# A spectral mixing layer with a gated MLP: the second-half sums of pair 0 move into the MLP, the first unit is reordered, statistics are issued sooner, and the DFT blocks get another layout

## The chip, the cores and the metric

The kernel runs on one core of a Trainium2 chip. The metric is the device time of one execution in microseconds; of several executions the median is taken.

## The reference

All arrays are fp32. x has 2048 rows (positions) of 512 values, F is 1792.

```python
xn = _layernorm(x, axis=-1)                       # eps 1e-5
a = einsum("bsd,ed->bse", xn, dft_hid_re)
b = einsum("bsd,ed->bse", xn, dft_hid_im)
s = einsum("ts,bse->bte", dft_seq_re, a) - einsum("ts,bse->bte", dft_seq_im, b)
g = sigmoid(einsum("bsd,df->bsf", xn, w_gate)) * einsum("bsd,df->bsf", xn, w_up)
out = x + s * silu(einsum("bsf,fd->bsd", g, w_down))
```

## The kernel before

Every matrix product is made of three fp32r products: each operand is split into a high part (a copy rounded to fp32r, on ScalarE, `high`, L120 or L373) and a low part (the operand less its high part, on VectorE, `make` or `low`, L125 or L376), and `mm3` adds high by high, low by high and high by low in PSUM. Large products are blocked two by two with seven products in place of eight (k = 1 to 7 in the code), at the price of sums and differences of blocks, on VectorE (`combine`, L129) or by adding DMAs.

The work runs in this order. First the transform along the sequence, in four chunks of 512 output positions (`Chunk`, t = 0 to 3); the hidden dimension follows later, at the end. Then the MLP, as 14 blocks of seven units for two halves of the positions (`block`, `Down`, `Seven`). Then the transform along the hidden dimension for two pairs of chunks (`hidden_units`), which multiplies the result by the gate and adds it to the output. Between them partial results stand in DRAM: f_raw (four blocks for each chunk), f_sum (sums of f_raw blocks of a pair of chunks, which `hidden_units` loads), g_part (the MLP's).

`units` is the list of all units of TensorE work. A unit of the sequence transform is 12 matmuls of 128x512; an MLP unit is 12, or 18 with a down product. The order is written by hand: for each unit n the loop at the end of the kernel issues what was hung on n by `sooner`, starts the loads of the units up to n + 5 (LOAD_AHEAD) and the splits of those up to n + 2 (SPLIT_AHEAD), then what hangs on n by `amid`, the unit itself, and what hangs on it by `after`. Each engine works through its own instructions in the order in which they are issued. All loads (`Load.load`, L81) go through SyncE's queue (SP), all stores and adding DMAs through GpSimd's. All tiles in SBUF that hold data are taken from one pool of 54 pages of 512 KB; a load whose page is still in use waits on its queue, with all behind it.

The first 24 units are products 1 and 2 of chunks 0 to 2 in turn (t runs fastest, then the pair of row blocks pp = 0 to 3). Their left operand is x normalised: `stats(0, pp)` finds mean and variance of a 128x2x512 tile on VectorE (L178, L179, L171) and the moments on GpSimd (L172 to L174, the one at L173 is a power of -0.5), `normed` (L370) normalises with them on ScalarE. e = 0, 1 are the two halves of a tile along its contraction; pair 0 and 1 are done in `begin`, pairs 2 and 3 by `prepare`, hung on units 6 and 9. Unit 0 has its own order of matmuls, in `Chunk.run`.

`n` in the driver is 112, the first unit of the MLP, so `f_sums(0, 1, n - 35, 2)` hangs four steps (L730: a sum on VectorE and its store) on units 77, 79, 81 and 83, with their loads of f_raw three units before. Units 84 to 111 are chunk 3. `x_norm` makes the transposed, normalised x of the MLP in the same time.

Of the kernel before, what the change touches and what calls it, by code (L numbers as in the profile page):

```python
# [11 lines left out]
ALU = mybir.AluOpType  # L12
ADD, SUB = ALU.add, ALU.subtract
# [19 lines left out]
def fnet_glu_kernel(ctx: ExitStack, tc: tile.TileContext, x, x_t, c_re, c_im, w_h, w_gu, w_down, out):  # L33
    nc = tc.nc
# [97 lines left out]
    units = []  # L132
# [9 lines left out]
    def sooner(n, f):  # L142
        early.setdefault(n, []).append(f)

    def amid(n, f):
        middle.setdefault(n, []).append(f)
# [15 lines left out]
    def moment(pp, m, j):  # L162
        return moments[:, pp, m, j, :]

    def stats(j, pp, apart=False):
        mv = stat.tile([P, 2, 2], F32, name="mv")
        rs = stat.tile([P, 2], F32, name="rs")

        def scale(e):
            mean, by, bias = (moment(pp, m, j)[:, e] for m in range(3))  # L170
            nc.vector.tensor_scalar(rs[:, e], mv[:, e, 1], EPS, None, op0=ALU.add)  # L171
            nc.gpsimd.tensor_tensor(mean, mv[:, e, 0], minus[:, e], op=ALU.mult)  # L172
            nc.gpsimd.tensor_tensor(by, rs[:, e], mhalf[:, e], op=ALU.pow)  # L173
            nc.gpsimd.tensor_tensor(bias, mean, by, op=ALU.mult)  # L174

        for e in range(2):
            st = stat.tile([P, 6], F32, name="st")
            nc.vector.bn_stats(st, xs[j, pp][:, e, :])  # L178
            nc.vector.bn_aggr(mv[:, e, :], st)  # L179
            if apart:  # L180
                scale(slice(e, e + 1))
        if not apart:
            scale(slice(0, 2))

    def normalise(j, pp, d=None):
        for e in range(2):
            v = xs[j, pp][:, e, :] if d is None else a_block(d, j, pp)[:, e]
            nc.scalar.activation(v, v, AF.Identity, scale=moment(pp, 1, j)[:, e : e + 1], bias=moment(pp, 2, j)[:, e : e + 1])
# [33 lines left out]


    def c_block(t, pp, j, m):
        v = (c_re, c_im)[m][t, j, pp]
        return Load(halves(v) if t < 2 and pp == j == m == 0 else v, [2, SB])

    class Sum(Value):
# [26 lines left out]
    class Chunk:  # L255
# [34 lines left out]
        def run(self, k, pp):  # L290
            ch = "p" if k < 3 and self.t < TOGETHER else CHAIN[k]
            if k in (1, 5) and pp == 0:
                self.chain(ch)
            wv, xv = aop[k, pp].get(), self.op[k, pp].get()
            turns = [(d, e, (0, 1, 2)) for d in range(2) for e in range(2)]
            if self.t < TOGETHER and k < 3:
                turns = [(d, e, (i,)) for i in range(3) for d in range(2) for e in range(2)]
                if (self.t, k, pp) == (0, 1, 0):
                    turns.sort(key=lambda v: (v[1], (0, 2, 1).index(v[2][0])))
                elif (self.t, k, pp) == (0, 1, 1):  # L300
                    turns.sort(key=lambda v: (v[2] == (2,), v[1], v[2]))
                elif (k, pp) == (1, 0):
                    turns.sort(key=lambda v: (v[2], v[1]))
            for d, e, only in turns:
                ws = [v[:, e, d * P : (d + 1) * P] for v in wv]
                first, last = k in (1, 5) and pp == e == 0, pp == 3 and e == 1
                mm3(self.ps[ch, d], ws, [v[:, e, :] for v in xv], first, last, k not in (1, 5), self.t > 0 or k < 3, only)
            if pp == 3:
                self.done(k)
# [51 lines left out]
    ready = []  # L361

    def tile_of(pp):
        a = aop[1, pp]
        both = page([2, 2, D // 2])
        a.at = both[:, 0], both[:, 1]
        return a.at, a_block(0, 0, pp)

    def normed(pp, to, src, e):
        nc.scalar.activation(to[:, e], src[:, e], AF.Identity, scale=moment(pp, 1, 0)[:, e : e + 1], bias=moment(pp, 2, 0)[:, e : e + 1])  # L370
# [4 lines left out]
    def low(parts, src, e=slice(0, 2)):  # L375
        nc.vector.tensor_tensor(parts[1][:, e], src[:, e], parts[0][:, e].bitcast(F32), op=SUB)  # L376
# [9 lines left out]
    def begin_seq():  # L386
        tags = {"p": "a", "c": "pd", "a": "a"}, {"p": "b", "c": "b", "a": "c"}, {"p": "c", "c": "pd", "a": "a"}, {"a": "c", "b": "a", "c": "pd"}
        chunks = [Chunk(t, tags[t], t in (1, 2)) for t in range(NT)]
        for i, k in enumerate((1, 2)):
            for pp in range(4):  # L390
                for c in chunks[:TOGETHER]:
                    add(c.needs(k, pp), lambda c=c, k=k, pp=pp: c.run(k, pp))
                m = TOGETHER * (4 * i + pp)
                if i:
                    sooner(m - 11, lambda pp=pp: fetch(1, pp))
                    after((6, 8, 10, 13)[pp], lambda pp=pp: stats(1, pp))
                    after((8, 10, 13, 16)[pp], lambda pp=pp: normalise(1, pp))
                else:
                    if pp > 1:
                        sooner(m - 3, lambda pp=pp: stats(0, pp))  # L400
                        sooner(m - 2, units[m][0][1].high)
                        sooner(m - 2, lambda pp=pp: ready.append(prepare(pp)))
                        amid(m - 2, lambda: low(*ready.pop()))
                    if pp > 2:
                        sooner(m - 9, lambda pp=pp: fetch(0, pp))
                    after(m + 2, lambda pp=pp: normalise(0, pp, 1))
                if i:
                    after(m + 2, lambda pp=pp: store_moments(pp))
        for pp in range(4):
            m = 4 * TOGETHER + TOGETHER * pp  # L410
            after(m - 3, lambda pp=pp: a_sums(pp, (1,)))
            after(20 + pp, lambda pp=pp: a_sums(pp, (3,)))
            after(m - 1, aop[5, pp].get)
            after(22 + pp, lambda pp=pp: a_sums(pp, (2,)))
            after(28 + pp, lambda pp=pp: a_sums(pp, (4,)))
        for c in chunks[:3]:
            for k in (5, 6, 7, 3, 4):
                c.add_product(k)
        for k in (1, 5, 6, 3, 7, 2, 4):
            chunks[3].add_product(k)  # L420
        return chunks

    def begin(chunks):
        for i, tag in enumerate(("gb", "ub", "pd", "pd")):
            idle = bank(tag)
            for _ in range((4, 4, 3, 2)[i]):
                nc.tensor.matmul(idle, ones[:, :P], ones, start=True, stop=True)
        first, second = (chunks[t].op[1, 0] for t in range(2))
        fetch(0, 0)
        for c in (first, second):  # L430
            c.raw = c.loads[0].at = page([2, SB], F32)
            c.parts = page([2, SB]), page([2, SB])
            for e in range(2):
                nc.sync.dma_start(c.raw[:, e, :], c.loads[0].src[:, e, :])
        fetch(0, 1)
        for n in (2, 3, 4):
            units[n][0][1].load()
        fetch(0, 2)
        units[5][0][1].load()
        stats(0, 0, True)  # L440
        a, src = tile_of(0)
        for e in range(2):
            high(first.parts, first.raw, e)
            normed(0, a[0], src, e)
            normed(0, src, src, e)
            low(first.parts, first.raw, e)
            low(a, src, e)
        first.at = first.parts
        for e in range(2):
            high(second.parts, second.raw, e)  # L450
        second.get()
        units[2][0][1].high()
        stats(0, 1, True)
        a, src = tile_of(1)
        normed(1, a[0], src, 0)
        normed(1, src, src, 0)
        units[2][0][1].get()
        low(a, src, 0)
        units[3][0][1].high()
        normed(1, a[0], src, 1)  # L460
        normed(1, src, src, 1)
        units[3][0][1].get()
        low(a, src, 1)
# [425 lines left out]
    with tc.manual_schedule():  # L889
        chunks = begin_seq()  # L890
        n = len(units)
# [10 lines left out]
        x_norm(1, 1, (n + 17, n + 20))  # L902
        x_ops(1, (n + 22, n + 24, n + 26, n + 27, n + 28, n + 30, n + 32, n + 33, n + 35, n + 36, n + 38))
        f_sums(0, 0, n - 46, 2)
        f_sums(0, 1, n - 35, 2)
        f_sums(1, 0, n + 54, 1)
        f_sums(1, 1, n + 70, 1)
        w_sums(n + 62)
# [30 lines left out]
def _layout(inputs):  # L939
    import numpy as np  # L940

    def seq(c):
        c = np.asarray(c).reshape(NT, SB, 4, P, 2, 2)
        v = c.transpose(0, 4, 2, 3, 5, 1).copy()
        return v

    def apart(blocks):
        for v in blocks:
            v[:] = v.transpose(1, 0, 2).copy().reshape(v.shape)
# [13 lines left out]

    x = np.asarray(inputs["A_x"]).reshape(NT, P, 2, 2, D).transpose(0, 2, 1, 3, 4).copy()
    c_re = seq(inputs["A_dft_seq_re"])
    apart([x[0, 0], c_re[0, 0, 0], c_re[1, 0, 0]])
    return {
        "x": x,
        "x_t": np.ascontiguousarray(
# [24 lines left out]
```

## Time and profile before

| what | value |
|---|---|
| time, three runs | 801.06 us median (800.4 to 801.15) |
| the profiled execution | 801.55 us, span of its instructions 799.8 us |
| granted TensorE clock | 0.999 |
| busy | TensorE 99%, weight loads 81%, VectorE 84%, ScalarE 65%, GpSimd 18% of the span |
| DMA | 182.07 MB in 53202 packets, mean 228 GB/s |

Times in the profile count from the start of the span. PE is TensorE, PEld its weight loads, DVE VectorE, ACT ScalarE, POOL GpSimd, SP SyncE. A row of the timeline gives start and length of a group of like instructions, engine, line, operation, out<-in, count, and in brackets the idle time of the engine ahead of it with what ended it. Matmuls are pipelined: one of 128x512 is shown with some 0.39 us, while the next starts after 0.23, so lost time is read from starts. DMA rows of a chain give the time from issue to landing.

### The profile page before, as it was taken

What the parts mean: (1) busy time and instruction counts of PE and PEld (TensorE: products, weight loads), DVE (VectorE), ACT (ScalarE), POOL (GpSimd) and SP (SyncE); (2) the same over time, 40 slices, a digit from 0 to 9 for tenths busy, and PEclk for the clock granted to TensorE, in tenths of its full rate; (3) what the DMA queues carried; (4) which work ended last, traced back from release to release, by engine and by line L of the source; (5) the groups of instructions that cost most, each with busy time, mean ns of one, the idle gap of its engine ahead of it and who ended that gap; (6) DMA issues with size and microseconds to landing.
All of it is one profiled execution on the core that took longest, in us unless ns stands there. A gap on an engine that the chain in (4) does not pass through costs nothing.

```text
span 799.8 us, 9917 instructions
## 1 busy us (share of the span) xinstructions
PE 789.0 (99%) x3469; PEld 650.0 (81%) x3469; DVE 669.0 (84%) x872; ACT 519.4 (65%) x792; POOL 141.0 (18%) x194
## 2 busy tenths in 40 slices
PE   9999999999998999999999999999999999999997
PEld 6788888888886888888888888888888888888886
DVE  6887999688887898899999867669869898896957
ACT  6795755534433555677877767676577787888471
POOL 2343000000111000213211111122222111112201
PEclk9999999999999999999999999999999999999999
DMA  9939763395799436949965974799999898999996
GB/s 344 408 117 291 182 251 145 126 321 193 272 350 372 127 107 220 266 145 239 211 129 98 175 149 106 204 225 287 288 299 258 191 226 220 232 284 311 301 330 106
DMA packets 53202, 182.07 MB, mean 228 GB/s; under 512 B 5920, under 2 KB 6176, under 8 KB 53152
## 3 DMA queue, kind: packets, MB, share of 16 engines
q0 software_dynamic: 23776, 78.67, 44.6%
q1 hardware_dynamic: 29296, 102.71, 35.1%
q8 instruction: 27, 0.44, 0.2%
q14 instruction: 23, 0.19, 0.1%
q10 hardware_dynamic: 80, 0.07, 0.0%
HBM read 114.29 MB, written 70.80 MB: 231 GB/s over the span
## 4 chain that ended last, share of the span: by engine, by line
PE 90%; DMA 5%; DVE 2%; ACT 1%; issue 1%; POOL 0%; SPq 0%; DVEq 0%; ACTq 0%
PE pd L72 25%; PE ga L72 16%; PE ua L72 16%; PE gc L72 11%; PE uc L72 11%; PE ub L72 6%; PE gb L72 6%; DMA page<-in_c_im_dram 3%; DMA page<-f_raw 2%; DVE page L125 1%; ACT page L370 1%; DMA page<-in_c_re_dram 1%; DVE page L129 0%; POOL moments L173 0%; DVE st L178 0%
## 5 line engine op out<-in xcount | busy, mean ns | idle before, releaser
L125 DVE TENSOR_TENSOR page<-page 128x1024 fp32r<-128x1024 f32 (+1 forms) x381 | 347.0, 941 | 72.9 <-ACT page L120 69.7
L120 ACT ACTIVATE page<-page 128x512 fp32r<-128x512 f32 (+1 forms) x380 | 299.7, 831 | 121.1 <-DVE page L129 91.0
L72 PE MATMUL pd<-page 128*128 128x512 f32 (+1 forms) x984 | 239.0, 387 | 1.3 <-DVE page L125 1.3
L72 PEld LDWEIGHTS pd<-page 128*128 128x128 f32 x984 | 183.0, 188 | 40.0 <-DVE page L125 2.6
L129 DVE TENSOR_TENSOR page<-page 128x1024 f32<-128x1024 f32 (+2 forms) x244 | 195.4, 820 | 3.2 <-DMA page<-in_c_im_dram 2.0
L72 PE MATMUL ga<-page 128*128 128x512 f32 x600 | 156.5, 390 | 1.1 <-DVE page L376 0.7
L72 PE MATMUL ua<-page 128*128 128x512 f32 x600 | 155.9, 389 | 0.0
L72 PEld LDWEIGHTS ga<-page 128*128 128x128 f32 x600 | 112.5, 188 | 26.6 <-DVE page L376 2.2
L72 PEld LDWEIGHTS ua<-page 128*128 128x128 f32 x600 | 112.7, 188 | 23.1
L543 POOL DMA_DIRECT2D g_part<-page x76 | 65.3, 864 | 269.5 <-ACT page L552 152.9
L72 PE MATMUL gc<-page 128*128 128x512 f32 x408 | 107.1, 390 | 1.2 <-ACT page L120 0.7
L72 PE MATMUL uc<-page 128*128 128x512 f32 x408 | 106.7, 389 | 0.0
L552 ACT ACTIVATE page<-pd 128x512 f32<-128x512 f32 x140 | 82.4, 598 | 24.8 <-PE pd L72 17.4
L72 PEld LDWEIGHTS gc<-page 128*128 128x128 f32 x408 | 76.4, 188 | 18.0 <-ACT page L120 1.1
L72 PEld LDWEIGHTS uc<-page 128*128 128x128 f32 x408 | 76.6, 188 | 15.9
L72 PE MATMUL gb<-page 128*128 128x512 f32 x228 | 61.0, 389 | 0.0
L72 PE MATMUL ub<-page 128*128 128x512 f32 x228 | 61.0, 389 | 0.0
L72 PEld LDWEIGHTS gb<-page 128*128 128x128 f32 x228 | 42.8, 188 | 8.9
L72 PEld LDWEIGHTS ub<-page 128*128 128x128 f32 x228 | 42.8, 188 | 8.9
L312 POOL DMA_DIRECT2D f_raw<-page x16 | 8.6, 540 | 179.4 <-DVE page L324 122.1
L660 ACT ACTIVATE page<-ga 128x512 f32<-128x512 f32 x28 | 16.6, 594 | 20.0 <-PE ga L72 18.2
L678 DVE TENSOR_TENSOR page<-page 128x512 f32<-128x512 f32 x28 | 19.3, 690 | 11.9 <-ACT page L675 11.3
(97 smaller groups left out, 379.6 us busy)
## 6 DMA issues: line engine op xcount, KB each, us to landing
g_part<-page POOLq DMA_DIRECT2D x84, 512.0 KB, 7.1
page<-in_c_re_dram SPq DMA_DIRECT2D x46, 512.0 KB, 7.3
page<-in_c_im_dram SPq DMA_DIRECT2D x32, 512.0 KB, 7.3
page<-f_raw SPq DMA_DIRECT2D x28, 512.0 KB, 7.8
page<-in_w_gu_dram SPq DMA_DIRECT2D x22, 512.0 KB, 6.4
f_raw<-page POOLq DMA_DIRECT2D x16, 512.0 KB, 5.4
f_sum<-page POOLq DMA_DIRECT2D x16, 512.0 KB, 7.7
page<-f_sum SPq DMA_DIRECT2D x16, 512.0 KB, 11.7
```

The costliest lines, as they stand in the source:

```text
L72: nc.tensor.matmul(ps, ws[w], ms[m], start=first and i == 0, stop=last and i == 2, skip_group_check=go_on)
L120: nc.scalar.activation(self.parts[0], self.raw, AF.Copy)
L125: nc.vector.tensor_tensor(lo, self.raw, hi.bitcast(F32), op=SUB)
L129: (engine or nc.vector).tensor_tensor(dst, a, b, op=op)
L312: nc.gpsimd.dma_start(f_raw[self.t][block], v)
L370: nc.scalar.activation(to[:, e], src[:, e], AF.Identity, scale=moment(pp, 1, 0)[:, e : e + 1], bias=moment(pp, 2, 0)[:, e : e + 1])
L543: nc.gpsimd.dma_start(g_part[i], pg, accum_op=ADD)
L552: nc.scalar.activation(pg[:, o, :], po, AF.Copy, scale=float(sign))
L660: nc.scalar.activation(s[k][:, m, :], ps[c + "a"], AF.Copy)
L678: nc.vector.tensor_mul(s[k][:, 0, :], s[k][:, 0, :], ps["u" + tag] if tag else s[k][:, 1, :])
```

## The change

It does five things. `f_sums(0, 1)` is hung on unit n + 38 = 150 with one unit between its steps, so on units 150 to 153 with loads on 147, 147, 148 and 150. In `begin`, half 0 of tile 0 is normalised on ScalarE ahead of the weight block, and the two halves of that tile get their exact value by `settle`, a subtraction and a multiplication in one instruction of VectorE, in place of a second pass of `normed`; unit 0 takes its matmuls in another order. x for pair 2 is loaded one block sooner. `stats(0, 2)` and `stats(0, 3)` hang one unit earlier and hand over each half by itself, and the low parts of pairs 2 and 3 are made half by half, with units 6 and 9 in the order that unit 3 has. The blocks of the sequence DFT lie in DRAM as [j, pp, t] instead of [t, j, pp].

```diff
     def c_block(t, pp, j, m):
-        v = (c_re, c_im)[m][t, j, pp]
+        v = (c_re, c_im)[m][j, pp, t]
...
                 if (self.t, k, pp) == (0, 1, 0):
-                    turns.sort(key=lambda v: (v[1], (0, 2, 1).index(v[2][0])))
-                elif (self.t, k, pp) == (0, 1, 1):
+                    order = (0, 0), (0, 1), (1, 0), (0, 2), (1, 2), (1, 1)
+                    turns.sort(key=lambda v: order.index((v[1], v[2][0])))
+                elif (self.t, k) == (0, 1):
                     turns.sort(key=lambda v: (v[2] == (2,), v[1], v[2]))
...
-                        sooner(m - 3, lambda pp=pp: stats(0, pp))
+                        sooner(m - 4, lambda pp=pp: stats(0, pp, True))
                         sooner(m - 2, units[m][0][1].high)
                         sooner(m - 2, lambda pp=pp: ready.append(prepare(pp)))
-                        amid(m - 2, lambda: low(*ready.pop()))
+                        for e in range(2):
+                            amid(m - 2, lambda e=e: low(*ready[-1], e))
...
         fetch(0, 1)
-        for n in (2, 3, 4):
+        for n in (2, 3):
             units[n][0][1].load()
         fetch(0, 2)
-        units[5][0][1].load()
-        stats(0, 0, True)
+        for n in (4, 5):
+            units[n][0][1].load()
+        mv = stats(0, 0, True)
         a, src = tile_of(0)
+
+        def settle(e):
+            v = src[:, e]
+            nc.vector.tensor_scalar(v, v, mv[:, e, 0:1], moment(0, 1, 0)[:, e : e + 1], op0=SUB, op1=ALU.mult)
+
+        normed(0, a[0], src, 0)
         for e in range(2):
             high(first.parts, first.raw, e)
-            normed(0, a[0], src, e)
-            normed(0, src, src, e)
+        settle(0)
+        low(a, src, 0)
+        settle(1)
+        high(a, src, 1)
+        for e in range(2):
             low(first.parts, first.raw, e)
-            low(a, src, e)
+        low(a, src, 1)
...
-        f_sums(0, 1, n - 35, 2)
+        f_sums(0, 1, n + 38, 1)
...
-        v = c.transpose(0, 4, 2, 3, 5, 1).copy()
+        v = c.transpose(4, 2, 0, 3, 5, 1).copy()
...
-    apart([x[0, 0], c_re[0, 0, 0], c_re[1, 0, 0]])
+    apart([x[0, 0], c_re[0, 0, 0], c_re[0, 0, 1]])
```

On ScalarE, at the start of the program (L370 is `normed`, L373 `high` of a weight block or of the tile, L120 `high` of a whole block), before:

```order
L373 ACTIVATE page<-page 128x512
L370 ACTIVATE page<-page,moments 128x256 x2
L373 ACTIVATE page<-page 128x512
L370 ACTIVATE page<-page,moments 128x256 x2
L373 ACTIVATE page<-page 128x512 x2
L120 ACTIVATE page<-page 128x1024
```

and now, two lines further down in the file (L372, L375):

```order
L372 ACTIVATE page<-page,moments 128x256
L375 ACTIVATE page<-page 128x512 x2
L375 ACTIVATE page<-page 128x256
L375 ACTIVATE page<-page 128x512 x2
L120 ACTIVATE page<-page 128x1024
```

One normalisation stands ahead of the first weight block, the three others are gone, and a copy of half 1 (128x256) stands behind both halves of the block.

On VectorE, around the statistics of pair 2 (L125 makes low parts of whole blocks, L376 those of a tile of x), before:

```order
L376 TENSOR_TENSOR page<-page 128x256
L125 TENSOR_TENSOR page<-page 128x1024
L178 BN_STATS st<-page 128x6
L179 BN_AGGR mv<-st 128x2
L178 BN_STATS st<-page 128x6
L179 BN_AGGR mv<-st 128x2
L171 TENSOR_SCALAR rs<-mv 128x2
L125 TENSOR_TENSOR page<-page 128x1024 x2
L376 TENSOR_TENSOR page<-page 128x512
```

and now (L378 is the former L376):

```order
L378 TENSOR_TENSOR page<-page 128x256
L178 BN_STATS st<-page 128x6
L179 BN_AGGR mv<-st 128x2
L171 TENSOR_SCALAR rs<-mv 128x1
L178 BN_STATS st<-page 128x6
L179 BN_AGGR mv<-st 128x2
L171 TENSOR_SCALAR rs<-mv 128x1
L125 TENSOR_TENSOR page<-page 128x1024 x3
L378 TENSOR_TENSOR page<-page 128x256 x2
```

The statistics stand ahead of one low part of a block that they stood behind, each half with its own hand-over, and the low part of pair 2's tile is made in two.

On SP's queue, the loads of units 74 to 85 (in_c_re and in_c_im are DFT blocks; f_raw_94, 98, 99 and 95 are what `f_sums(0, 1)` reads; in_x_t and m_part belong to `x_norm`), before:

```order
L81 DMA page<-in_c_re_dram 128x1024
L81 DMA page<-f_raw_94 128x1024
L81 DMA page<-f_raw_98 128x1024
L81 DMA page<-in_c_re_dram 128x1024 x2
L81 DMA page<-in_x_t_dram 128x1024
L81 DMA page<-f_raw_99 128x1024
L81 DMA page<-in_c_re_dram 128x1024
L81 DMA page<-m_part0b 128x512
L81 DMA page<-in_x_t_dram 128x1024
L81 DMA page<-in_c_re_dram 128x1024
L81 DMA page<-f_raw_95 128x1024
L81 DMA page<-in_c_re_dram 128x1024 x2
```

and now the same loads in the MLP, among those of its weights:

```order
L81 DMA page<-in_w_gu_dram 128x1024 x2
L81 DMA page<-in_w_down_dram 128x1024
L81 DMA page<-f_raw_94 128x1024
L81 DMA page<-f_raw_98 128x1024
L81 DMA page<-f_raw_99 128x1024
L81 DMA page<-in_w_gu_dram 128x1024 x2
L81 DMA page<-f_raw_95 128x1024
L81 DMA page<-in_w_down_dram 128x1024
```

The four loads have left the stretch ahead of chunk 3; three of them stand ahead of a pair of gate weights now. Their four stores moved on GpSimd's queue in the same way, each behind one of the MLP's g_part stores.

More of the change, by code (lines that the diff above doesn't have):

```diff
@@ L183, in stats @@
             scale(slice(0, 2))
+        return mv
     def normalise(j, pp, d=None):
```

## The prediction

> **What bounds the kernel now.** I read the page's busy times first, then TensorE's waits, then the timeline around each wait.
>
> ```profile
> PE 789.0 (99%) x3469; PEld 650.0 (81%) x3469; DVE 669.0 (84%) x872; ACT 519.4 (65%) x792; POOL 141.0 (18%) x194
> ```
>
> TensorE is busy for 789.0 of 799.8 us, so a change that leaves its 3469 matmuls alone can win only what TensorE loses to waits. The list of its waits (engine, tile, who released it, us, times, longest) is short, and these are its longest:
>
> ```profile
> PE pd L72 <- DVE page L125: 1.3, 3, 0.7
> PE ga L72 <- DVE page L376: 0.7, 1, 0.7
> ```
>
> The timeline of TensorE shows where most of them lie (start us, us, group, xcount, idle before it).
>
> ```profile
> 242.96 1.52 PE L72 MATMUL gc<-page 128*128 128x512 f32 x6
> 244.32 1.52 PE L72 MATMUL uc<-page 128*128 128x512 f32 x6
> 246.53 0.73 PE L72 MATMUL gc<-page 128*128 128x512 f32 x2 [0.69 <-ACT page L120]
> 247.79 1.20 PE L72 MATMUL gc<-page 128*128 128x512 f32 x4 [0.53 <-DVE page L125]
> 248.82 1.53 PE L72 MATMUL uc<-page 128*128 128x512 f32 x6
> 250.20 0.61 PE L72 MATMUL pd<-page 128*128 128x512 f32 x2
> 251.19 3.06 PE L72 MATMUL pd<-page 128*128 128x512 f32 x12 [0.38 <-DVE page L125]
> 254.96 5.78 PE L72 MATMUL pd<-page 128*128 128x512 f32 x24 [0.71 <-DVE page L125]
> 260.93 2.56 PE L72 MATMUL pd<-page 128*128 128x512 f32 x10 [0.19 <-DVE page L125]
> 263.33 1.52 PE L72 MATMUL gc<-page 128*128 128x512 f32 x6
> ```
>
> Six matmuls without a wait take 244.32 - 242.96 = 1.36 us, 0.2267 each. From 244.32 to 263.33 there are 66, worth 14.96 us; they took 19.01. This stretch, the start of the last chunk of the sequence transform, loses **4.05 us**. The idle times in brackets add up to less, since a matmul after a wait also starts the next one 0.11 us late. The engines named are not the cause: the chain of waits leads from them to transfers, each of which is long in landing, and over 215 to 262 us the transfers run at the rate of the third row.
>
> ```profile
> 222.98 12.05 DMA page<-f_raw
> 235.09 20.00 DMA page<-in_c_im_dram
> ...
> DMA packets 5047, 15.99 MB, mean 340 GB/s; under 512 B 518, under 2 KB 518, under 8 KB 5045
> ```
>
> A load issued at 235.09 lands 20 us later: the transfers are backed up, and the f_raw load in this chain is one of those that the change moves. The other losses are at the start.
>
> ```profile
> 7.00 0.50 PE L72 MATMUL ga<-page 128*128 128x512 f32 x1 [0.36 <-ACT page L370]
> ...
> 10.32 0.40 PE L72 MATMUL gb<-page 128*128 128x512 f32 x1
> ...
> 15.80 0.41 PE L72 MATMUL ga<-page 128*128 128x512 f32 x1
> ...
> 18.80 0.40 PE L72 MATMUL gb<-page 128*128 128x512 f32 x1
> ...
> 24.26 0.62 PE L72 MATMUL ga<-page 128*128 128x512 f32 x2
> ...
> 27.99 0.62 PE L72 MATMUL gb<-page 128*128 128x512 f32 x2
> ```
>
> A unit has 12 matmuls, 2.72 us. Unit 0 (7.00 to 10.32) takes 3.32, unit 3 (15.80 to 18.80) 3.00, unit 6 (24.26 to 27.99) 3.73: losses of 0.60, **0.28** and **1.01** us.
>
> **The change part by part.** First, pair 0's second-half sums. They leave the stretch before 245 us with four loads, four stores and four additions. At 340 GB/s a transfer of 512 KB (0.524 MB) takes 1.54 us of all queues. Seven of the eight were served before the first wait (the fourth store was issued last): 10.8 us of transfers that stand ahead of what TensorE waits for. What must come earlier is 4.05 us, plus what TensorE gains at the start (1.6, below), 5.7 in all. 10.8 covers it, so I take all of 4.05; the ends are 0 (the loads then wait for pages instead) and 4.05. The additions cost VectorE 1.22 each, the first row here, which also shows it waiting for a load.
>
> ```profile
> 242.90 1.22 DVE L129 TENSOR_TENSOR page<-page 128x1024 f32<-128x1024 f32 x1 [0.41 <-DMA page<-in_c_im_dram]
> ```
>
> With 4.9 us of additions gone VectorE has room there too: next late would be its own pace, two operations of 1.22 in a unit of 2.72.
>
> The new place are units 147 to 153. Unit 92 begins at 263.33; 28 units of 12 matmuls and 27 of 18 (4.08 us) later is 450. There the same work meets this (columns: busy PE, PEld, DVE, ACT, POOL; clock; DMA share; GB/s):
>
> ```profile
> 450.00:460.00 10.00, 10.00 (x46) 8.29 (x45) 9.04 (x13) 8.40 (x15) 1.70 (x2) 1.00 0.99 219
> 460.00:470.00 10.00, 10.00 (x46) 8.29 (x45) 6.62 (x10) 6.02 (x11) 1.70 (x2) 1.00 0.60 109
> ...
> 540.00:550.00 10.00, 10.00 (x46) 8.29 (x45) 9.90 (x15) 5.26 (x11) 2.14 (x4) 1.00 1.00 284
> ```
>
> The queues are not empty there, but the last row is a part of the MLP in which the same kind of sums (pair 1's) already run with the transfers at 1.00 and VectorE at 9.90, and TensorE holds its 46 matmuls in 10 us. VectorE has 3.4 us free in 460 to 470 and the additions come one in a unit of 18 matmuls (4.08 us). On SP's queue two loads of gate weights stand behind three of the moved loads, on GpSimd's three stores of partial results behind three of the moved stores; both queues run units ahead of TensorE. I cost the new place at 0, with TensorE's lead as cover, and at 1 to 3 us if that cover is gone.
>
> Second, the first unit. Its work on ScalarE, VectorE and GpSimd:
>
> ```profile
> 5.83 0.63 ACT L373 ACTIVATE page<-page 128x512 fp32r<-128x512 f32 x1 [3.59 <-DMA page<-in_c_re_dram]
> 6.37 1.22 ACT L370 ACTIVATE page<-page,moments 128x256 fp32r<-128x256 f32 x2
> 9.14 1.14 ACT L373 ACTIVATE page<-page 128x512 fp32r<-128x512 f32 x2
> ...
> 5.85 0.15 DVE L171 TENSOR_SCALAR rs<-mv 128x1 f32<-128x1 f32 x1
> 9.27 0.42 DVE L376 TENSOR_TENSOR page<-page 128x256 fp32r<-128x256 f32 x1 [0.43 <-ACT page L370]
> 10.31 1.23 DVE L125 TENSOR_TENSOR page<-page 128x1024 fp32r<-128x1024 f32 x1 [0.62 <-ACT page L373]
> ...
> 5.11 0.19 POOL L174 TENSOR_TENSOR moments<-moments 128x1 f32<-128x1 f32 x1
> 6.08 0.56 POOL L173 TENSOR_TENSOR moments<-rs,mhalf 128x1 f32<-128x1 f32 x1
> 20.89 1.62 POOL L173 TENSOR_TENSOR moments<-rs,mhalf 128x2 f32<-128x2 f32 x1
> ```
>
> ScalarE now normalises half 0 as soon as its moments stand, at 5.30, instead of after the weight block: done at 5.9. The block's high part follows (0.63) to 6.50, and TensorE starts at 6.55 rather than 7.00. Half 1 is longer: it goes through settle on VectorE. A TENSOR_SCALAR of 128x256 is not in the trace; it costs between 0.15 (the same operation at 128x1) and 0.42 (the same width with two tensors), and I take 0.42, the row of its width. settle(0) runs 6.00 to 6.42, the low part to 6.84. GpSimd's power for half 1 would start at 6.08; the row at 20.89 shows what it takes while VectorE adds or subtracts, 1.62 instead of 0.56. I let it wait for settle(0): 6.42 + 0.56 = 6.98. settle(1) ends at 7.42, the copy on ScalarE (0.58) at 8.03, and TensorE, out of work by then, goes on with half 1 at 8.08. Eight matmuls and 0.11 later unit 1 starts at 10.0 instead of 10.32: **0.32**. The other end, 0.15 and no wait on GpSimd, has half 1 at 7.7 and unit 1 at 9.65, a gain of 0.67; should the copy come 0.4 later than I put it, the gain is below 0.
>
> The Trainium skill (SBUF — State Buffer, Who interferes with whom) says that a tensor_scalar can enter a mode that holds the port pair shared with GpSimd for the whole instruction, and that a two-input operation blocks GpSimd's reads. The row at 20.89 agrees for the two-input kind; if settle held nothing, half 1 would start 0.16 sooner and the gain be 0.48. The Trainium skill (VectorE: DVE Perf Modes, the perf-mode tier table) gives fp32 tensor_scalar in SBUF twice the rate of tensor_tensor; by its figure settle takes about 0.29 (an estimate), and the gain would be 0.59 with the block.
>
> Third, the statistics. ScalarE does one normalisation instead of four ahead of the second weight block; three of 0.6 us go, one copy comes, and the block's last half is there by about 8 us:
>
> ```profile
> page<-in_c_re_dram SPq DMA_DIRECT2D x4, 256.0 KB, 4.4
> ```
>
> (issued by 3.5, 4.4 to landing). Its high parts end near 9.0 instead of 10.28, so VectorE's subtraction at 10.31 and all of pair 1 behind it come 1.2 earlier, while TensorE reaches unit 3 only 0.3 earlier. Unit 3 waited 0.28; that goes with 0.6 to spare. For pair 2 the statistics stood behind unit 4's subtraction and their power took 1.62; now they come a unit earlier and in halves, and their input is requested one block sooner. Next late is the weight block of unit 6:
>
> ```profile
> 19.90 1.06 ACT L120 ACTIVATE page<-page 128x1024 fp32r<-128x1024 f32 x1 [0.23 <-DMA page<-in_c_re_dram]
> ```
>
> After it come the four normalisations, at most 2.44 (twice the two at 6.37), to 23.4; the low halves are there by 23.3 and 23.8. Unit 6 starts at 24.26 - 0.32 - 0.28 = 23.7 and needs them two and six matmuls later, at 24.1 and 25.0: its 1.01 goes. If the moments are still late, it stays. The statistics for pair 3 take VectorE 2 us ahead of unit 7's low part, which TensorE needs only in the last third of that unit.
>
> Fourth, the layout. It changes which addresses a block has, not its size. The trace has loads of blocks in both kinds of order, one after the other without a pause: from 20 to 40 us blocks that lie eight apart, from 256.4 to 259.4 blocks that lie side by side (last two columns: DMA share, GB/s).
>
> ```profile
> 20.00:40.00 20.00, 19.29 (x85) 15.57 (x84) 16.54 (x29) 15.56 (x24) 7.83 (x12) 1.00 1.02 408
> 256.40:259.40 3.00, 3.00 (x15) 2.47 (x14) 3.00 (x3) 1.04 (x1) 1.22 (x1) 1.00 1.03 408
> ```
>
> 408 GB/s in both: I cost the order at 0.
>
> The sum: 4.05 + 0.32 + 0.28 + 1.01 = 5.66. The profiled execution took 801.55 us (span 799.8), 0.49 over the median of the three runs, 801.06. 801.06 - 5.66 = **795.4**; against the profiled one, 795.9.
>
> **The rivals.** (a) A rest stays in the first units: unit 6 still waits or the copy of half 1 is late. Then 0.4 to 1.3 us less is won, 795.8 to 796.7. For it: pair 2's chain runs through three engines. (b) The stretch at 245 keeps half of its loss, because loads are held by pages that come free with TensorE, not by the queue: 797.4. Against it: 235.09 to 255.09 is time after the issue. (c) The MLP pays 1 to 3 us: 796.4 to 798.4. For it: 0.99 in 450 to 460. (d) Slower: the moved stores hold pages that ScalarE writes next. A row of the waits of ScalarE elsewhere in the MLP shows such a case,
>
> ```profile
> ACT page L660 <- DMA f_sum<-page: 0.4, 1, 0.4
> ```
>
> of 0.4. If each of the four stores held ScalarE and, behind it, TensorE for more than 5.66 / 4 = 1.4 us, the kernel is slower; at 12 us to landing, as the f_raw load took in the backlog, and a lead of two units (SPLIT_AHEAD), 8 us, it is 4 x 4 = 16, 811. Against it: 0.4 is small, and TensorE did not wait there. (e) The layout or a page hold undoes the gain at 245 wholly: 799.5.
>
> **How the numbers follow.** The forecast 0.62; (a) 0.13, (b) 0.08, (c) 0.11, (d) 0.03, (e) 0.03. The forecast's own spread is 794.6 (all of the ends, and 0.4 of scatter below the median) to 796.2. The range 794.6 to 797.6 takes (a) and most of (b) and (c). About 0.2%, 1.6 us, is what a measurement can tell. Faster by more: 0.93, the forecast, (a), (b) and nearly all of (c); within 0.2%: 0.04, (e) and the end of (c); slower: 0.03, (d).
>
> **What would show it.** In the profile after: no wait of TensorE between 240 and 265 us, and loads there that land within some 6 us of their issue; TensorE's first real matmul at 6.55, unit 1 near 10.0, no idle time in units 3 and 6; 45 or 46 matmuls in every 10 us of 440 to 500. Wrong would be: a wait of ScalarE for f_sum in the MLP with TensorE behind it, a 20 us landing that stays, or a first unit that ends after 10.32.

## The result, and the profile after

The changed kernel takes **795.54 us** in the median of six runs (795.47 to 796.19), the kernel before 801.11 (six runs, 800.4 to 802.96): a ratio of 0.993, 95% interval 0.9917 to 0.9942, or 5.6 us less. 795.4 was forecast. The profiled execution took 795.55 us, its span is 793.8.

The first part of the page after, the busy times, and below it TensorE's whole list of waits (engine, tile, who released it, us, times, longest):

```profile
PE 786.7 (99%) x3469; PEld 651.4 (82%) x3469; DVE 669.1 (84%) x878; ACT 517.9 (65%) x790; POOL 144.5 (18%) x200
...
PE gb L430 <- DVE ones L50: 1.5, 1, 1.5
```

The one wait left is that of the first warm-up matmul for its constant; the list of before has it too, and it was the longest there, not the two that the prediction shows as the longest. From its first real matmul on TensorE waits for nothing. The stretch before the last chunk, from the timeline of TensorE, from the table of windows (busy PE, PEld, DVE, ACT, POOL; clock; DMA share; GB/s) and from the list of transfers between 215 and 262 us:

```profile
246.51 11.04 PE L72 MATMUL pd<-page 128*128 128x512 f32 x48
...
230.00:245.00 15.00, 15.00 (x68) 12.43 (x67) 10.18 (x10) 5.22 (x6) 2.98 (x3) 1.00 1.06 352
245.00:262.00 17.00, 17.00 (x77) 14.08 (x76) 15.85 (x15) 10.19 (x12) 0.00 (x0) 1.00 0.40 104
...
DMA packets 3846, 11.64 MB, mean 248 GB/s; under 512 B 372, under 2 KB 372, under 8 KB 3843
...
page<-in_c_im_dram SPq DMA_DIRECT2D x8, 512.0 KB, 9.9
```

48 matmuls that stood in four pieces (2, 12, 24 and 10) run without a break. 4.35 MB less is moved (15.99 before). The queues are still full up to 245 (share 1.06) but drained by 262 (0.40), and a load of in_c_im lands 9.9 us after its issue in the median. The same row of before:

```profile
page<-in_c_im_dram SPq DMA_DIRECT2D x8, 512.0 KB, 16.8
```

The start, from the timelines of TensorE, VectorE and GpSimd:

```profile
5.04 2.23 PE L430 MATMUL pd<-ones 128*128 128x512 f32 x5
7.11 0.39 PE L72 MATMUL ga<-page 128*128 128x512 f32 x1
...
9.87 0.39 PE L72 MATMUL gb<-page 128*128 128x512 f32 x1
...
15.31 0.39 PE L72 MATMUL ga<-page 128*128 128x512 f32 x1
...
18.03 0.62 PE L72 MATMUL gb<-page 128*128 128x512 f32 x2
...
23.47 0.39 PE L72 MATMUL ga<-page 128*128 128x512 f32 x1
...
26.19 0.62 PE L72 MATMUL gb<-page 128*128 128x512 f32 x2
...
5.94 0.41 DVE L449 TENSOR_SCALAR page<-page,mv,moments 128x256 f32<-128x256 f32 x1 [0.55 <-ACT page L372]
...
5.47 0.56 POOL L173 TENSOR_TENSOR moments<-rs,mhalf 128x1 f32<-128x1 f32 x1
```

Units 0, 3 and 6 now take 2.76 (7.11 to 9.87), 2.72 and 2.72 us, where they took 3.32, 3.00 and 3.73. Unit 1 begins at 9.87 instead of 10.32. But the first real matmul comes at 7.11, not sooner than before (7.00): the warm-up matmuls in front of it kept their slow pace longer.

At the sums' new place, from ScalarE's waits between 430 and 520 us and from the windows there (450 to 460 us also has 45 matmuls):

```profile
ACT page L120 <- DMA g_part<-page: 2.4, 2, 2.0
...
460.00:470.00 10.00, 10.00 (x45) 8.26 (x44) 6.49 (x10) 7.42 (x14) 3.52 (x5) 1.00 0.96 197
```

ScalarE waits 2.4 us for pages that stores of partial results (g_part) still read. The list of before has no such entry in this time. TensorE does not feel it: 45 matmuls in 10 us.

### The profile page after: what moved, and what is told of

Read it like the earlier page. It is cut to its first block, busy times and chain, and to the rows that moved or that the text cites. A ratio compares the mean times of both kernels' runs of the same rounds, so it can differ in the third digit from the quotient of the medians.

```text
span 793.8 us, 9918 instructions
## 1 busy us (share of the span) xinstructions
PE 786.7 (99%) x3469; PEld 651.4 (82%) x3469; DVE 669.1 (84%) x878; ACT 517.9 (65%) x790; POOL 144.5 (18%) x200
## 4 chain that ended last, share of the span: by engine, by line
PE 99%; DVE 0%; issue 0%
PE pd L72 28%; PE ga L72 17%; PE ua L72 17%; PE uc L72 12%; PE gc L72 12%; PE ub L72 7%; PE gb L72 7%; PE gb L430 0%; PE pd L430 0%; PE ub L430 0%; DVE page L871 0%; DVE page L872 0%; DVE ones L50 0%
## 5 line engine op out<-in xcount | busy, mean ns | idle before, releaser
L125 DVE TENSOR_TENSOR page<-page 128x1024 fp32r<-128x1024 f32 (+1 forms) x381 | 346.4, 940 | 73.3 <-ACT page L120 71.7
L120 ACT ACTIVATE page<-page 128x512 fp32r<-128x512 f32 (+1 forms) x380 | 299.2, 830 | 113.4 <-DVE page L129 93.1
L673 ACT ACTIVATE page<-ga 128x512 f32<-128x512 f32 x28 | 16.6, 593 | 17.6 <-PE ga L72 16.2
```

The source lines that it names most:

```text
L120: nc.scalar.activation(self.parts[0], self.raw, AF.Copy)
L125: nc.vector.tensor_tensor(lo, self.raw, hi.bitcast(F32), op=SUB)
L673: nc.scalar.activation(s[k][:, m, :], ps[c + "a"], AF.Copy)
```

## The experiments

Each ran in 5 or 11 executions (the second run of the old first unit in one) beside the kernel before, in three groups of four runs, each group on a chip of its own. The median of before was 800.70 us in the first group (21 runs), 801.31 in the second (9) and 801.31 in the third (15). The changed kernel itself did not run beside them, so the comparisons with its 795.54 go across chips; runs that turned out to cost nothing stand for it in each group: 795.63 in the first, 795.40 and 795.72 in the second, 795.75 in the third. The theory: the bytes of the moved sums stood in the queues ahead of loads that TensorE needs. Its rivals: the additions on VectorE, and pages that the sums hold.

**The move alone.** The kernel before with the one line:

```diff
-        f_sums(0, 1, n - 35, 2)
+        f_sums(0, 1, n + 38, 1)
```

> The kernel before with one line changed: the second-half sums of pair 0 hang on unit n + 38. My step: all of the 4.05 us of the stretch before 263 goes and nothing is paid in the MLP, 801.1 - 4.05 = 797.0, with the waits at units 0, 3 and 6 as before. Rival (pages hold the loads, not the queue): half, 799.1. Rival (the MLP pays): 798 to 800, with TensorE waits between 440 and 500 us.

797.37 us (796.95 to 797.83), ratio 0.9955 (0.9943 to 0.9968): 3.3 us less than the 800.70 beside it. The 48 matmuls run as one, and nothing is waited for in the MLP:

```profile
248.50 11.04 PE L72 MATMUL pd<-page 128*128 128x512 f32 x48
```

**The move undone.** The changed kernel with the old line.

> The changed kernel with its second-half sums of pair 0 back at unit n - 35. If the parts simply add, 795.5 + 4.05 = 799.6. If the transfers of the stretch keep their times while TensorE arrives 1.7 us sooner, the stretch takes the start's gain as well, and the time is 801.2: then the start is worth nothing without the move.

799.26 us (798.75 to 800.06), ratio 0.9978 (0.997 to 0.9987): 3.7 over the changed kernel's 795.54. TensorE's timeline has the waits again, the longest of them here:

```profile
252.30 5.73 PE L72 MATMUL pd<-page 128*128 128x512 f32 x24 [0.77 <-DVE page L125]
```

The parts add: what is left without the move is the start's own gain, 801.11 - 799.26 = 1.85, or 1.44 against the 800.70 beside it. The stretch does not swallow it, though TensorE arrives there sooner.

**The transfers alone.** The changed kernel, and where the sums stood:

```diff
+        for i, (t, b, o) in enumerate(((0, 0, 0), (1, 0, 0), (1, 1, 2), (0, 1, 6))):
+            v = Load(f_raw[t][b], [2, SB])
+            sooner(n - 38 + o, v.load)
+            after(n - 35 + 2 * i, lambda i=i, v=v: nc.gpsimd.dma_start(junk[i], v.load()))
```

> The changed kernel with four loads of the same f_raw blocks and four stores (to four spare arrays) added where the sums stood before, without the additions on VectorE. Theory queue: the transfers alone bring the loss back, 799.6 to 801.2, with TensorE waiting between 244 and 263. Theory VectorE: 795.5 and no wait.

799.41 us (798.48 to 800.73): the whole loss, 3.9, without any addition. TensorE's timeline, the window, a row of ScalarE's timeline and one of the transfers from 200 to 262:

```profile
232.79 1.20 PE L74 MATMUL ga<-page 128*128 128x512 f32 x4 [2.11 <-DVE page L127]
233.83 1.54 PE L74 MATMUL ua<-page 128*128 128x512 f32 x6
235.21 1.52 PE L74 MATMUL ga<-page 128*128 128x512 f32 x6
...
245.00:262.00 17.00, 15.95 (x68) 12.18 (x67) 15.40 (x14) 7.55 (x10) 1.22 (x1) 1.00 0.96 305
...
230.96 1.06 ACT L122 ACTIVATE page<-page 128x1024 fp32r<-128x1024 f32 x1 [3.21 <-DMA page<-in_c_re_dram]
...
junk<-page POOLq DMA_DIRECT2D x4, 512.0 KB, 14.2
```

VectorE is again the engine named (L127 and L122 are the former L125 and L120). What VectorE itself waited for before it went on at 231.51 the profile does not say; in the same time ScalarE stood 3.21 us for a load, to 230.96. The window shows the queues at 0.96 after 245. The size of the loss is that of the move undone, its place only in part: 2.1 us go at 232, where that run does not wait, and waits between 249 and 260 come back.

**The additions alone.**

```diff
+        for i in range(8):
+            after(n - 35 + 2 * (i // 2), lambda: nc.vector.tensor_tensor(ones, ones.bitcast(F32), ones.bitcast(F32), op=ALU.mult))
```

> The changed kernel with the additions alone added where the sums stood before: eight of 128x512 on VectorE, on a constant, no transfers and no pages. Theory queue: 795.5, no wait of TensorE. Theory VectorE: the loss is back, 799.6. A mixture would stand between, with TensorE waiting for VectorE at 244 to 263.

795.63 us (795.46 to 795.9). Eight operations, 5.6 us by the timeline of VectorE (the first of four pairs here), and TensorE waits for nothing:

```profile
218.07 1.41 DVE L920 TENSOR_TENSOR ones<-ones 128x512 fp32r<-128x512 f32 x2
```

The theory of VectorE's time falls.

**The pages alone.** As the run with transfers alone, but with each load and store cut to a sixteenth:

```diff
+            nc.sync.dma_start(held[i][:, :, :32], f_raw[t][b][:, :, :32])
...
+            after(n - 35 + 2 * i, lambda i=i: nc.gpsimd.dma_start(junk[i][:, :, :32], held[i][:, :, :32]))
```

> The four spare loads and stores of the run with transfers alone, each cut to 32 of 512 columns (a sixteenth of the bytes), with the same four pages held between the same instructions. Theory queue time (the bytes ahead of the loads that TensorE needs): 795.5, at most 0.3 more. Theory pages (what the sums cost is that they hold pages that loads wait for): 799.4 as with the whole transfers, TensorE waiting between 230 and 260.

795.40 us (795.14 to 795.48). The small stores still take 10.4 us to land, against 14.2 of the whole ones, so the pages are held most of the time that they were. ScalarE even stands 5.93 us for such a page, and TensorE waits for nothing:

```profile
226.46 2.96 ACT L122 ACTIVATE page<-page 128x1024 fp32r<-128x1024 f32 x3 [5.93 <-DMA junk<-page]
...
junk<-page POOLq DMA_DIRECT2D x4, 32.0 KB, 10.4
```

It is the bytes. Whether a part of their price comes by way of pages, held some 4 us longer by whole stores, these runs do not separate.

**Half of the bytes.** The same with the loads whole and the stores small.

> As the run with four spare loads and stores in the stretch, but the loads whole (512 KB) and the stores cut to 32 of 512 columns: half of the bytes. If the loss grows evenly with the bytes, half of 3.9 comes back, 797.4. If there is a slack that the first bytes use up (my step had 10.8 us of transfers against 5.7 needed), half of them costs little, 795.5 to 796.0. If loads cost more than stores because they stand in SyncE's queue ahead of the loads that TensorE needs, up to 799.

797.19 us (795.56 to 798.05). Four executions took 797.2 to 798.1; the profiled one took 795.56, and in it TensorE does not wait:

```profile
page<-in_c_im_dram SPq DMA_DIRECT2D x8, 512.0 KB, 13.1
...
245.00:262.00 17.00, 17.00 (x76) 14.08 (x75) 16.35 (x15) 9.98 (x12) 1.20 (x1) 1.00 0.67 204
```

A landing of 13.1 us is in the middle between 9.9 and 16.8, and the median in the middle between 795.5 and 799.4. Half of the bytes may be about where this stretch begins to wait, some executions over it and some not; where the others waited was not traced, so that is not shown.

**The statistics undone.**

```diff
-                        sooner(m - 4, lambda pp=pp: stats(0, pp, True))
+                        sooner(m - 3, lambda pp=pp: stats(0, pp))
...
-                        for e in range(2):
-                            amid(m - 2, lambda e=e: low(*ready[-1], e))
+                        amid(m - 2, lambda: low(*ready.pop()))
...
-                elif (self.t, k) == (0, 1):
+                elif (self.t, k, pp) == (0, 1, 1):
```

> The changed kernel with the statistics of pairs 2 and 3 one unit later and for both halves at once, low parts joined, units 6 and 9 in their former order; x is still requested one block sooner. My step: unit 6 waits 1.01 again, 796.5. Rival: the earlier request of x and the shorter start of ScalarE are enough, 795.5.

796.67 us (795.97 to 797.14): 1.1 over the changed kernel, and 0.8 in the traced execution (796.35). In the timelines of TensorE and GpSimd unit 6 waits for its low part again, unit 7 begins at 26.90 instead of 26.19, and the power for both halves at once again takes 1.63 us beside VectorE's subtraction:

```profile
24.95 0.72 PE L72 MATMUL ga<-page 128*128 128x512 f32 x2 [0.38 <-DVE page L378]
...
26.90 0.63 PE L72 MATMUL gb<-page 128*128 128x512 f32 x2
...
19.54 1.63 POOL L173 TENSOR_TENSOR moments<-rs,mhalf 128x2 f32<-128x2 f32 x1
```

**The first unit undone**, in two runs of the same kernel. `begin` normalises twice on ScalarE as before, without `settle`, and unit 0 has its former order.

```diff
-        normed(0, a[0], src, 0)
         for e in range(2):
             high(first.parts, first.raw, e)
-        settle(0)
...
+            normed(0, a[0], src, e)
+            normed(0, src, src, e)
             low(first.parts, first.raw, e)
-        low(a, src, 1)
+            low(a, src, e)
```

> The changed kernel with the first unit as before (both passes of the normalisation on ScalarE, its old order of matmuls). My step: 0.32 for unit 0 and 0.28 for unit 3, 796.1; with the 0.55 that the traces now give unit 0, 796.4. Rival: the later units have the slack to take it up, 795.5. TensorE in unit 0: 3.3 us instead of 2.8.

> The kernel with the old first unit once more, for a second trace: its profiled run took 796.11, while the other four took 796.9 to 797.2. If a wait that is there in some executions costs the 1.0 between, a trace near 797.1 shows it at units 1 to 7 (theory: unit 6's weight block or moments) and nowhere after 30 us.

797.08 us (796.11 to 797.17), and 795.94 for the second. Starts of the first real matmul and of units 1, 3, 4 and 6 in the first trace, then of units 1 and 6 in the second:

```profile
6.80 0.50 PE L72 MATMUL ga<-page 128*128 128x512 f32 x1 [0.40 <-ACT page L371]
...
10.11 0.39 PE L72 MATMUL gb<-page 128*128 128x512 f32 x1
...
15.61 0.40 PE L72 MATMUL ga<-page 128*128 128x512 f32 x1
...
18.60 0.62 PE L72 MATMUL gb<-page 128*128 128x512 f32 x2
...
24.06 0.39 PE L72 MATMUL ga<-page 128*128 128x512 f32 x1
```

```profile
9.87 0.39 PE L72 MATMUL gb<-page 128*128 128x512 f32 x1
...
23.76 0.39 PE L72 MATMUL ga<-page 128*128 128x512 f32 x1
```

In the first trace the old order costs 0.24 by unit 1, unit 3 takes 2.99 us instead of 2.72 (15.61 to 18.60), and unit 6 begins 0.59 later than in the changed kernel (24.06 against 23.47). In the second the warm-up was slow, the operands were all there when it ended, and unit 1 begins at 9.87 as in the changed kernel; small delays follow, and unit 6 begins 0.29 later (23.76). The two traced executions took 0.56 and 0.39 more than that of the changed kernel, so the first units account for most of it. The four executions without a trace took 796.9 to 797.2, which neither trace shows. What they waited for stays open.

**The old layout**, on the changed kernel: `[m][t, j, pp]` and its transposition in the host's arrays.

> The changed kernel with the DFT blocks in their former order in DRAM. My step: the order of the blocks costs nothing, 795.5, and the loads before 262 us land as soon. Rival: the order sets the rate of the loads, then the stretch before 262 shows longer landings and a wait, 796 to 797.

795.72 us (795.44 to 796.36) against 795.54 (795.47 to 796.19): the same.

**The moved work doubled.** On the units 150 to 153 the changed kernel does four more loads, additions and stores:

```diff
+        for i, (t, b) in enumerate(((0, 0), (1, 0), (1, 1), (0, 1))):
+            v = Load(f_raw[t][b], [2, SB])
+            sooner(n + 35 + i, v.load)
+            after(n + 38 + i, lambda i=i, v=v: nc.gpsimd.dma_start(junk[i], combine(v.load(), v.load(), v.load(), ADD)))
```

> The changed kernel with the moved work in the MLP doubled: four more loads of f_raw, additions and stores (to spare arrays) on the same units 150 to 153. Theory cover (TensorE's lead hides them): 795.5, no wait of TensorE, though ScalarE's waits for stores grow over the 2.4 us that it has now. Rival (the cover is nearly used up): 796.5 to 799, with waits of TensorE between 440 and 500.

801.39 us (799.73 to 803.16), ratio to before 1.0003 (0.9992 to 1.0013): all that the change won is gone again, 5.8 us, beyond either expectation. From ScalarE's waits between 430 and 475 us, ScalarE's timeline, TensorE's timeline and the windows (two lines further down L120 is L122, L673 is L675):

```profile
ACT page L122 <- DMA g_part<-page: 9.5, 4, 4.3
...
466.78 0.63 ACT L122 ACTIVATE page<-page 128x512 fp32r<-128x512 f32 x1 [4.32 <-DMA g_part<-page]
467.32 0.58 ACT L675 ACTIVATE page<-ga 128x512 f32<-128x512 f32 x1
...
467.95 2.93 PE L74 MATMUL ga<-page 128*128 128x512 f32 x6 [2.53 <-ACT page L675]
470.67 1.86 PE L74 MATMUL ua<-page 128*128 128x512 f32 x6
...
468.00:472.00 4.00, 4.00 (x11) 3.22 (x12) 4.00 (x6) 2.92 (x6) 1.53 (x3) 0.58 0.84 262
```

The rows read as a chain. A store of partial results is late: those between 440 and 475 us take 8.1 us to land in the median, against 6.4 in the changed kernel. ScalarE wants to write a high part into its page and stands for 4.32 us. Behind it in ScalarE's order stands the copy that empties bank ga (L675, 467.32), and TensorE stands for that bank until 467.95. Afterwards the granted clock is 0.58, and six matmuls take 470.67 - 467.95 = 2.72 us where six take 1.36. The traced execution took 5.3 us more than that of the changed kernel; this wait and another of 0.75 are 3.3 of them, the slow matmuls behind it 1.7. This is rival (d)'s mechanism, a store that holds the page that ScalarE writes next, with one difference: the store is not one of those that were moved or added, but one of g_part that shares the queues with them.

**Two warm-up matmuls fewer**, a version that might have beaten both:

```diff
-            for _ in range((4, 4, 3, 2)[i]):
+            for _ in range((4, 4, 2, 1)[i]):
```

> The changed kernel with 11 warm-up matmuls on ones instead of 13. If the warm-up holds unit 0 (first real matmul at 7.11 where its operands were there by 6.4), the first real matmul comes at 6.5 to 6.7. But half 1 then holds it: in the runs whose warm-up ended sooner its matmuls began at 7.84 to 7.89, so unit 1 starts at 9.75 instead of 9.87 and the time is 795.4, not to be told from 795.5. Rival (no such second hold): 795.0.

795.75 us (795.71 to 795.95): nothing is won. TensorE's timeline:

```profile
6.80 0.80 PE L72 MATMUL ga<-page 128*128 128x512 f32 x1 [0.28 <-ACT page L375]
7.39 0.52 PE L72 MATMUL ua<-page 128*128 128x512 f32 x1
...
10.03 0.39 PE L72 MATMUL gb<-page 128*128 128x512 f32 x1
```

The first real matmul comes at 6.80, but it is slow itself (0.59 to the next one), and unit 1 begins no sooner. No version here beats the changed kernel.

## Why the prediction was right

**The stretch before 263, 4.05 us: right, a little too large.** The move is worth 3.3 us by itself and 3.7 in the changed kernel, and the runs with transfers, additions and pages apart show that the bytes do it. In the trace of the move alone the 66 matmuls of the stretch take their 14.96 us (244.42 to 259.38), so there all of the 4.05 goes; it was read from an execution 0.49 above the median, and the medians gain less. The working behind it was less good. It held 10.8 us of transfers against 5.7 needed, a slack by which half of them could have stayed. With half of them the median lost 1.65 (797.19 - 795.54), though the one traced execution lost nothing: hardly slack, if the others waited in this stretch. And the loads do not land within 6 us, but in 9.9: the queues stay full to 245, only less far behind.

**The new place at 0: right for this dose, by a reason that did not carry.** I took a row in which pair 1's sums run beside TensorE for a proof of cover. It showed that the cover held there, not how thick it is here. ScalarE's wait of 2.4 us was a warning of rival (d), and the doubled dose costs 5.8. The 16 us that I gave that rival came from a wrong price for each store. Its place was right, and its chain but for the store at its head: I had the moved stores hold the pages, and it was one of g_part.

**The first unit, 0.32: the size came out (0.45 in the trace), two steps did not.** The first failing step is "TensorE starts at 6.55": the data were there, the warm-up matmuls were not done. They hold a pace of 0.427 us (5.04, 5.47, 5.89 and so on in the trace) up to 6.75 here, and left it at about 5.5 in the trace of before. The second is GpSimd's power for half 1, which I let wait for `settle`; x had landed earlier and the power ran at 5.47, before it. That half 1 comes late, as I had it, is seen where the warm-up ended sooner, as in the run with the move undone: first real matmul at 6.67, half 1 after a wait of 0.13 at 7.84, and unit 1 at 9.77. So the two limits lie next to each other. In the ten traces with the new order unit 1 starts at 9.75 to 10.03, in the four with the old one at 9.87 to 10.42: the forecast of 10.0 instead of 10.32 lies within what single executions scatter, and 0.45 is one pair of them. What the new order is worth apart from this stays between 0.4 (two traces' times, 795.94 and 796.11) and 1.5 (the median of the first of the two runs).

```profile
6.67 0.51 PE L72 MATMUL ga<-page 128*128 128x512 f32 x1 [0.34 <-ACT page L375]
...
7.84 0.50 PE L72 MATMUL ga<-page 128*128 128x512 f32 x1
...
9.77 0.39 PE L72 MATMUL gb<-page 128*128 128x512 f32 x1
```

**The statistics, 1.01: right in kind.** Undone, they cost 1.1 in the median, with the wait at unit 6, but 0.7 of it in the trace (26.90 against 26.19) and not 1.01. The earlier request of x for pair 2 stays in that run; what it is worth by itself is not shown.

**Unit 3, 0.28: right.** With the first unit as before, in the first of its traces, unit 3 loses 0.27 again (2.99 against 2.72). There the start as a whole costs 0.59, where the terms for units 0 and 3 add up to 0.60; in the second trace it costs 0.29.

**The layout at 0: right**, 0.2 with both ranges over one another.

The sum, 5.66 against 5.57 measured, owes some of its accuracy to luck: by the medians the stretch gave some 0.3 to 0.7 less, and the start up to 0.2 more than its terms (1.85 against 1.61). Between the two profiled executions the difference is 6.00, with 1.80 of it by unit 7 (27.99 to 26.19).

## What to carry to other kernels

A wait that names VectorE can be a queue full of bytes: add the transfers, the additions and the page holds one at a time, and see which of them brings the loss back. Work moved to a place without waits can use up cover that the profile shows only on another engine; look for new short waits there (2.4 us on ScalarE here), since twice the work cost as much as the whole change had won. The start of a kernel can be set by two limits side by side, and then taking one away wins little; and one trace of a start is one sample of it.

## What the runs showed of the hardware

**`settle` costs what a subtraction costs.** TENSOR_SCALAR of 128x256 fp32 took 0.41 to 0.43 us, as the TENSOR_TENSOR of that width (0.42). The Trainium skill (VectorE: DVE Perf Modes, the perf-mode tier table) has it at twice the rate, 0.29 as an estimate; the trace does not agree.

**It holds GpSimd in some executions and not in others.** Beside the first `settle` GpSimd has a product of 128x1 (L174). Rows of GpSimd and VectorE, first of the run with the additions alone, then of before, where a subtraction with two tensors stands in that place:

```profile
6.27 0.19 POOL L174 TENSOR_TENSOR moments<-moments 128x1 f32<-128x1 f32 x1
...
6.17 0.43 DVE L449 TENSOR_SCALAR page<-page,mv,moments 128x256 f32<-128x256 f32 x1 [0.62 <-ACT page L372]
```

```profile
6.72 0.51 POOL L174 TENSOR_TENSOR moments<-moments 128x1 f32<-128x1 f32 x1
...
6.49 0.69 DVE L376 TENSOR_TENSOR page<-page 128x512 fp32r<-128x512 f32 x1 [0.49 <-ACT page L373]
```

And of the changed kernel, where the `settle` beside it is the row at 5.94 above:

```profile
6.11 0.29 POOL L174 TENSOR_TENSOR moments<-moments 128x1 f32<-128x1 f32 x1
```

In the first the product runs inside `settle` in its usual 0.19 us. In before it ends 0.05 after the subtraction (7.23 and 7.18), and in the changed kernel just so after `settle` (6.40 and 6.35). Of the ten traces with `settle` six are like the last, with `settle` at 0.41 us, and four like the first, with `settle` at 0.43. What decides between the two is not shown.

**The clock fell after a wait of 2.5 us.** With the doubled work TensorE stood 2.53 us, and the granted clock was 0.58 over the next 4 us: six matmuls took 2.72 us, 1.36 more than six without a wait, so the wait cost over half as much again as itself. In the run with transfers alone a wait of 2.11 us left no such trace: six matmuls from 233.83 to 235.21, 1.38 us. The Trainium skill (TensorE: Matmul & The Clock Gate, Why this matters for your kernels) asks for no idle gap over about 3 us; here a shorter one was enough. Another wait, of 0.75 us, stood 7 us ahead of it; whether that had a part was not tried.

**The end of the warm-up moves from execution to execution.** The first warm-up matmul starts at 1.46 in all fourteen traces, and the pace of 0.427 us ends at 5.0 in the run with the move undone and not before 6.75 in the changed kernel, 3.5 and 5.3 us later.

```profile
5.01 1.32 PE L430 MATMUL pd<-ones 128*128 128x512 f32 x5
```

Here five matmuls take about as long as three do at the slow pace; in the row of the changed kernel the five took 2.23. The Trainium skill (TensorE: Matmul & The Clock Gate, Part 1: The HAM clock gate) puts the change at about 4 us of matmuls, half a microsecond more or less run to run, and says that the window behind it is not started by the kernel. The traces agree with the second and show a wider spread than the first.
